# Coarse scores in four array quarters, coarse transposes in row halves, and a new opening order in a two-scale attention kernel

## The chip, the cores and the metric

The kernel runs on one core of one Trainium2 chip. The metric is the device time of one execution in microseconds (us). The engines are TensorE (PE, with its weight loads PEld), VectorE (DVE), ScalarE (ACT), GpSimd (POOL) and the queue SP, which only starts transfers.

## The reference

For 8 batches, 8 heads, 576 positions and a head dimension of 64:

```python
q_d, k_d, v_d = (t.reshape(B, H, 144, 4, D).mean(axis=3) for t in (q, k, v))
out_d = softmax(q_d @ k_d.T / 8) @ v_d                # coarse scale
out_up = repeat(out_d, 4, axis=2)
scores = where(abs(i - j) < 4, q @ k.T / 8, -1e9)     # local band
x = out_up + softmax(scores) @ v                      # heads joined to 512 columns
gate = sigmoid(sum(conv_w[k] * shifted(x, k) for k in range(5)))
out = (gate * (x @ w_val)) @ w_out
```

Weights come in as float64, the rest as float32.

## The kernel before

Work is cut into 32 pairs of heads, four to a batch; `p` counts pairs. For each pair TensorE makes: local scores (`sl`, a mask product and 40 small products), coarse scores (`sd`, six products of 64 rows by 64 columns by 144), transposes of the local weights (`tl0`, `tl1`) and of the coarse weights (`tc0`, `tc1`), the local values (`x`, 20 products) and the coarse values (`odp`). A product in float32 is two records in the trace (288 records on `sd` of 24 pairs). DVE takes the maxima (`mx`, `cmx`), subtracts, sums, adds local and coarse parts (`xt`) and does the convolution taps (`gp`); ACT does the exponentials and copies results out of PSUM (`pt`, `pdt`, `od`, `xh`, `hh`, `ob`); POOL shares the pooling, some normalisations and low parts (`xl`, `hl`) with DVE.

Behind the pairs run two projections in split precision: `val` = x by `w_val` and `out` = h by `w_out`, 256 chunks of six products (lines 864 to 866). The text calls a chunk P, as the order strings do. A chunk of `val` needs `xh` and `xl` of two pairs of its batch.

The coarse means of q and k come, for the first eight pairs, from DVE and POOL (`half`, `qd`); later ones, and all means of v, are summed by transfers: one load (`qs0`, `vs0`) and three accumulating transfers that POOL starts (line 401). `odp` of a batch waits for the third (`vs3`).

What sets the order: on TensorE two strings written out by hand. `FILL` gives the first ten pairs, 41 chunks among them; after it `STEADY` is repeated for each pair. On the other engines a planner orders operations by due times and lengths, with corrections by name (`BIAS`) and by instance (`DUE`). Each engine runs its list in order. Filler products (`keep_warm`, line 374) are put where the planner expects TensorE to stand idle.

PSUM has eight banks: three in rotation under the tag `s` (`sl`, `sd`, and two for `x`), two under `t` (`tl`, `tc`, `odp`), three under `v`. An operation that takes a bank waits until its last user has been read.

Of the kernel before, what the change touches and what calls it, by code (L numbers as in the profile page):

```python
# [8 lines left out]
F32 = mybir.dt.float32  # L9
# [28 lines left out]
LATE = {"qs": 9000, "vs": 7000}  # L38
# [3 lines left out]
ROWS, NG, GR = 112, 3, 48  # L42

LO, HI = slice(0, 64), slice(64, 128)
SB, TB, VB = 3, 2, 3
# [18 lines left out]
)  # L64
STEADY = "P P sl tc1' tc0' sd tl1' tl0' P P P P P P odp' x'"
# [5 lines left out]
    "pdt1": -8000, "h2.0": 2000, "hlo3.0": -1000, "norm1": 2000, "fld": 4000, "h2.1": -8000, "h3.0": -4000,  # L71
    "cwfld": 2000, "xl": -8000, "pvb": 2000, "od": -1000, "xt0": -2000, "exp": 1000, "rcp": -2000,
    "cexp0": -1000, "h1.1": 4000, "cmx0": -1000, "hhi3.0": -2000,
}
FIRST = {("qk", 0): -2e6, ("qk2", 0): -1.9e6}
DUE = {("raw", 0): -799008, ("vw", 0): -799729, ("raw", 2): 10251, ("qk", 1): -799570}
# [6 lines left out]
class Planner:  # L83
# [5 lines left out]
    LOAD = 1000  # L89
# [36 lines left out]
    def lat(self, o):  # L126
        return o["late"] or (self.LOAD if "SP" in o["opts"] else self.LAT)

# [34 lines left out]
    def simulate(self):  # L163
# [3 lines left out]
        self.recent, self.idle, self.port = [], {}, 0  # L167
# [17 lines left out]
        while events:  # L185
# [127 lines left out]
def tile_two_scale_attn_gated_conv(  # L313
# [9 lines left out]
    mask: bass.AP,  # L323
    out: bass.AP,
# [13 lines left out]
    ident = cpool.tile([P, P], F32, name="ident")  # L338
    ident_b = cpool.tile([P, P], BF16, name="ident_b")
# [31 lines left out]
    def keep_warm(bank):  # L371
        n = min(WARM, bank.shape[1])
        for _ in range(plan.warm):
            nc.tensor.matmul(
                out=bank[:, 0:n],
                lhsT=nc.const_aps.tensor(1.0, (P, bank.shape[0]), BF16),
                rhs=nc.const_aps.tensor(1.0, (P, n), BF16),
                start=True,
                stop=True,
            )  # L380
# [9 lines left out]
    def sums_in(b):  # L390
# [25 lines left out]
    def load(p):  # L416
# [670 lines left out]
```

## Time and profile before

| | |
|---|---|
| three runs | 419.21 us median, 416.21 to 419.66 |
| span of the profiled execution | 412.6 us |
| that execution's own time | not listed apart: the median is 6.6 us over the span, the fastest run 3.6 us |
| PE busy | 387.2 us, 94% |
| DVE, ACT, POOL busy | 306.3, 251.3, 140.4 us |
| moved by transfers | 68.00 MB, mean 165 GB/s |

The span runs from the first to the last instruction; what lies around it is in the runs' times and not in the profile. Busy shares are averages over an opening, a long regular stretch and a tail, so they are read by stretch. A PE record lasts longer than its slot, since products overlap: how long a step takes is the distance from its start to the start of the next step.

### The profile page before, as it was taken

To read this page: it belongs to the slowest core of one execution; us is meant where nothing else is said; L and a number is where in the kernel's file an instruction comes from. 1 tells how busy PE (TensorE), PEld (TensorE's weight loads), DVE (VectorE), ACT (ScalarE), POOL (GpSimd) and SP (SyncE) were. 2 spreads that over 40 slices of the span, in tenths; PEclk is the share of its full clock that TensorE was granted. 3 is DMA by queue.
4 is the path that set the end of the run, shared out by engine and by line. 5 is a ranking of instruction groups with operands and counts; after the bars stand their busy time and mean duration, and the time that the engine had idled before them with its cause. 6 is when DMAs were issued, how large, how long until landed. Compare 5 with 4: busy or idle time off the path is not lost.

```text
span 412.6 us, 15125 instructions
## 1 busy us (share of the span) xinstructions
PE 387.2 (94%) x6505; PEld 342.8 (83%) x6505; DVE 306.3 (74%) x650; ACT 251.3 (61%) x693; POOL 140.4 (34%) x159
## 2 busy tenths in 40 slices
PE   8664888989999999999999999999999999999996
PEld 5444656879998988888999989888888999998996
DVE  2676869989998976786689678786678668974730
ACT  1445677579667675566656665676556665675321
POOL 4563484365443322541154213432254112320000
PEclk9688698999999999999999999999999999999999
DMA  7987778668796479846994798667894431001002
GB/s 225 279 189 206 223 208 228 124 195 249 187 211 146 152 210 237 192 108 171 257 217 88 209 234 221 160 173 215 231 176 96 150 126 40 20 30 59 31 30 86
DMA packets 23603, 68.00 MB, mean 165 GB/s; under 512 B 3056, under 2 KB 4080, under 8 KB 23536
## 3 DMA queue, kind: packets, MB, share of 16 engines
q1 hardware_dynamic: 18352, 49.17, 36.7%
q0 software_dynamic: 4896, 17.70, 25.6%
q8 instruction: 51, 0.84, 0.8%
q10 hardware_dynamic: 288, 0.16, 0.1%
q14 instruction: 16, 0.13, 0.1%
HBM read 57.59 MB, written 9.44 MB: 162 GB/s over the span
## 4 chain that ended last, share of the span: by engine, by line
PE 82%; DMA 6%; DVE 5%; POOL 2%; ACT 2%; issue 1%; SPq 0%; ACTq 0%; POOLq 0%; DVEq 0%
PE out L864 9%; PE val L864 9%; PE out L865 8%; PE out L866 8%; PE val L866 8%; PE val L865 8%; PE sd L549 6%; PE sl L482 5%; PE x L671 5%; PE tl L621 5%; PE tc L644 5%; PE odp L708 5%; DMA raw_v<-in_w_val 3%; DMA qk<-in_qk 3%; PE sl L475 1%
## 5 line engine op out<-in xcount | busy, mean ns | idle before, releaser
L753 DVE SCALAR_TENSOR_TENSOR gp<-xt,cw,gp 128x576 f32<-128x576 f32 x128 | 109.8, 858 | 0.5 <-ACT gp L747 0.2
L864 PE MATMUL val<-xh,wh_v 128*128 128x288 f32 x256 | 79.4, 310 | 0.0
L864 PE MATMUL out<-hh,wh_o 128*128 128x288 f32 x256 | 78.8, 308 | 0.0
L866 PE MATMUL val<-xl,wh_v 128*128 128x288 f32 x256 | 76.0, 297 | 1.4 <-issue 1.1
L865 PE MATMUL val<-xh,wl_v 128*128 128x288 f32 x256 | 75.9, 297 | 0.0
L865 PE MATMUL out<-hh,wl_o 128*128 128x288 f32 x256 | 75.7, 296 | 0.0
L866 PE MATMUL out<-hl,wh_o 128*128 128x288 f32 x256 | 75.6, 295 | 0.0
L518 POOL TENSOR_TENSOR pexp<-ex,rs 64x350 f32<-64x350 f32 x38 | 44.1, 1159 | 78.5 <-DVE crs L587 26.5
L682 DVE TENSOR_TENSOR xt<-x,od 128x290 f32<-128x290 f32 x64 | 26.7, 452 | 37.1 <-PE x L671 35.9
L866 PEld LDWEIGHTS val<-xl,wh_v 128*128 128x128 f32 x256 | 48.4, 189 | 2.1 <-issue 1.3
L864 PEld LDWEIGHTS val<-xh,wh_v 128*128 128x128 f32 x256 | 48.4, 189 | 1.4 <-issue 0.4
L864 PEld LDWEIGHTS out<-hh,wh_o 128*128 128x128 f32 x256 | 48.1, 188 | 1.1 <-issue 0.2
L865 PEld LDWEIGHTS val<-xh,wl_v 128*128 128x128 f32 x256 | 48.5, 189 | 0.0
L865 PEld LDWEIGHTS out<-hh,wl_o 128*128 128x128 f32 x256 | 48.2, 188 | 0.0
L947 ACT ACTIVATE ob<-out 128x288 f32<-128x288 f32 x64 | 26.1, 407 | 36.3 <-PE out L866 33.2
L866 PEld LDWEIGHTS out<-hl,wh_o 128*128 128x128 f32 x256 | 48.0, 188 | 0.0
L626 ACT COPY pt<-tl 128x256 f32<-128x256 f32 (+1 forms) x64 | 25.9, 425 | 19.4 <-PE tl L621 19.4
L401 POOL DMA_DIRECT2D vs<-in_vgr x24 | 20.5, 865 | 47.6 <-PE sd L549 20.7
L571 ACT ACTIVATE pd<-sd,cbi 112x144 f32<-112x144 f32 x96 | 35.3, 376 | 1.8 <-DVE cbi L564 1.7
L651 ACT COPY pdt<-tc 72x336 f32<-72x336 f32 x64 | 25.2, 434 | 17.3 <-PE tc L644 17.2
L401 POOL DMA_DIRECT2D qs<-in_qkr x18 | 18.1, 1006 | 51.6 <-DMA qs<-in_qkr 24.6
L621 PE MATMUL tl<-ident,pexp 128*128 128x128 f32 x160 | 26.5, 290 | 8.9 <-POOL pexp L518 4.7
(83 smaller groups left out, 758.8 us busy)
## 6 DMA issues: line engine op xcount, KB each, us to landing
qk<-in_qk SPq DMA_DIRECT2D x31, 586.0 KB, 5.7
qs<-in_qkr POOLq DMA_DIRECT2D x18, 576.0 KB, 7.4
vw<-in_vw SPq DMA_DIRECT2D x32, 320.0 KB, 4.9
out_t<-ob SPq DMA_DIRECT2D x31, 288.0 KB, 3.7
vs<-in_vgr POOLq DMA_DIRECT2D x24, 288.0 KB, 5.5
qs<-in_qkr SPq DMA_DIRECT2D x6, 576.0 KB, 5.8
vs<-in_vgr SPq DMA_DIRECT2D x8, 288.0 KB
raw_v<-in_w_val SPq DMA_DIRECT2D x8, 256.0 KB, 4.7
```

What stands on the lines that cost most here:

```text
L401: nc.gpsimd.dma_start(out=u[nm][:, cs], in_=src[b, r][:, cs], accum_op=ALU.add)
L518: eng.tensor_tensor(out=px[r, :, BQ * e : BQ * e + KW], in0=s["ex"][r, :, 0:KW], in1=s["rs"][r].broadcast_to([64, NSB, KW]), op=ALU.mult,)
L571: nc.scalar.activation(out=s["pd"][:, g], in_=s["sd"][:, g], func=AF.Exp, scale=1.0 / 128.0, bias=s["bi"][:, g : g + 1], accum_out=s["csm" ...
L621: nc.tensor.transpose(out=tp[:, j], in_=s["px"][:, m : m + 2].rearrange("p a b -> p (a b)"), identity=ident)
L626: nc.scalar.copy(out=s["pt"][:, lo : lo + n], in_=s["tl", u])
L651: nc.scalar.copy(out=s["pdt"][:, kb], in_=s["tc", kb])
L682: nc.vector.tensor_tensor(out=s["xt"][:, 4:].rearrange("p (m a j r) -> p a m j r", m=NPR, a=2, r=2)[:, par], in0=s["x", par].rearrange("p ...
L753: nc.vector.scalar_tensor_tensor(out=s["gp"], in0=s["xt"][:, k : k + S], scalar=cw[:, c, k : k + 1], in1=s["gp"], op0=ALU.mult, op1=ALU.add,)
L864: nc.tensor.matmul(out=o, lhsT=wh[:, d, col], rhs=his[d][:, cs], start=d == 0, stop=False)
L865: nc.tensor.matmul(out=o, lhsT=wl[:, d, col], rhs=his[d][:, cs], start=False, stop=False)
L866: nc.tensor.matmul(out=o, lhsT=wh[:, d, col], rhs=los[d][:, cs], start=False, stop=d == NC - 1)
L947: nc.scalar.mul(t["ob"][:, cs], box[hf][:, ps_cs], 0.5)
```

## The change

- **Coarse scores.** The six products go to two banks at three places of 256 columns, in an order in which four neighbouring products use four different quarters of the array (rows low or high, columns low or high), then two more. Before, three rounds of two.
- **Coarse transposes.** `tc0` and `tc1` become one step `tc` of twelve transposes, each of 48 rows by 72 columns, low rows and high rows in turn, into two banks of tag `t`; the six before took 112 rows. ACT copies 288 columns twice in place of 336.
- **First batch's means of v.** A new step `vd` for pairs 0 to 3: six products of a constant 0/1 matrix (`pick`, 221 KB, loaded once) with the values already on chip, and an ACT copy. The load and three accumulating transfers of that batch are gone.
- **Banks.** Tag `s` keeps one bank for `sl`; a new tag `w`, one buffer of two banks, is shared by `sd` and `x`.
- **Order.** `FILL`, `BIAS` and `DUE` have new values, the planner's model of transfers is changed, and fillers before `tl` and `odp` use float32 ones.

```diff
-LATE = {"qs": 9000, "vs": 7000}
+LATE = {"qs": 2930, "vs": 1480}
+PLACE = (0, 2, 1, 0, 2, 1)
-SB, TB, VB = 3, 2, 3
+TB, VB = 2, 3
 FILL = (
-    "sl:0 sd:0 tl1:0 tc0:0 sl:1 tc1:0 sd:1 tl1:1 tl0:0 sl:2 sd:3 tc0:1 tc1:1 tl0:1 sl:4 odp:1 odp:0 sl:3 "
-    "x:1 tl1:2 x:0 sd:2 tl0:2 tc1:3 tl1:3 tl0:3 sd:4 x:2 tc0:2 tc1:2 odp:2 tl1:4 sl:5 P tc0:3 odp:3 tc1:4 "
-    "sd:5 x:3 tl0:4 P tc0:4 P P tc1:5 P P P sd:6 P x:4 P P odp:4 sl:6 tl0:5 P P tc1:6 tc0:6 P P sl:7 "
...
+    "sl:0 sd:0 sl:1 sd:1 tl0:0 tc:0 tl1:1 vd:0 sl:2 tl1:0 odp:0 sd:3 tc:1 tl0:1 vd:1 tl1:2 sl:4 odp:1 x:1 "
+    "sl:3 x:0 sd:2 P tl0:2 tl0:3 tl1:3 sd:4 x:2 tc:2 tl0:4 P vd:2 vd:3 odp:2 tl1:4 sl:5 tc:3 P x:3 odp:3 tc:4 "
+    "sd:5 tl1:5 P P P P sd:6 P odp:4 P sl:6 tc:5 P P odp:5 x:4 tc:6 sl:7 sd:7 odp:6 tl0:5 P P P sl:8 tl0:6 P "
...
-STEADY = "P P sl tc1' tc0' sd tl1' tl0' P P P P P P odp' x'"
+STEADY = "P P sl tc' sd tl1' tl0' P P P P P P odp' x'"
 BIAS = {
-    "pdt1": -8000, "h2.0": 2000, "hlo3.0": -1000, "norm1": 2000, "fld": 4000, "h2.1": -8000, "h3.0": -4000,
+    "pdt1": -6000, "h2.0": 5000, "hlo3.0": -9000, "norm1": 18000, "fld": 21000, "h2.1": -7000,
...
-            ("vs", vgr, [SD // 2, NC, 4, D], "odp", 820, 0),
+            ("vs", vgr, [SD // 2, NC, 4, D], "odp", 1100, 0 if b else NC),
...
-            sc = ps.tile([P, 3, SD], F32, tag="s", name=f"sd{p}", bufs=SB)
-            keep_warm(sc.rearrange("p a b -> p (a b)"))
+            w = ps.tile([P, 2, 512], F32, tag="w", name=f"sd{p}", bufs=1).rearrange("p a b -> p (a b)")
+            sc = w[:, 0:768].rearrange("p (i j) -> p i j", j=256)[:, :, 0:SD]
+            keep_warm(w[:, 0:512])
             q = s["qd"].rearrange("p a j -> p (a j)")
-            for i in range(3):
-                for r in (LO, HI):
-                    nc.tensor.matmul(
-                        out=sc[r, i],
-                        lhsT=q[r, 48 * i : 48 * i + 64],
+            for u in (0, 1, 4, 5, 2, 3):
+                h, j = divmod(u, 3)
+                r = LO if h == 0 else HI
+                nc.tensor.matmul(
+                    out=sc[HI if u % 2 else LO, PLACE[u]],
+                    lhsT=q[r, 48 * j : 48 * j + 64],
...
-    def coarse_transpose(p, kb):
+    def coarse_transpose(p):
...
+            for kb in range(2):
+                for n in range(NG):
+                    for e, r in enumerate((slice(0, GR), slice(64, 64 + GR))):
+                        nc.tensor.transpose(
+                            out=tps[e][:, kb, n],
+                            in_=s["pd"][r, PLACE[2 * n + e], half * kb : half * kb + half],
+                            identity=ident[r, r],
+                        )
...
+        for e in range(2):
+            op((f"pdt{e}", p), "ACT", 335, evac(e), [("tc", p)], free=[("odp", p - 2)])
...
+            w = ps.tile([P, 2, 512], F32, tag="w", name=f"x{p}", bufs=1)
             for par in range(2):
-                s["x", par] = ps.tile([P, NPR * GQ], F32, tag="s", name=f"x{par}_{p}", bufs=SB)
+                s["x", par] = w[:, par, 0 : NPR * GQ]
...
+    def value_sums(p):
...
+            for kb in range(2):
+                for n in range(3):
+                    nc.tensor.matmul(
+                        out=t[:, kb],
+                        lhsT=pick[:, 3 * kb + n],
+                        rhs=s["vw"][:, 2 * kb + n].rearrange("p h d -> p (h d)"),
+                        start=n == 0,
+                        stop=n == 2,
+                    )
...
+        op(("vd", p), "PE", 1330, mm, [("vw", p), ("pick", 0)], banks=[("t", [("vdc", p)])], cols=(3072, 256))
+        op(("vdc", p), "ACT", 320, evac, [("vd", p)])
```

**TensorE, one pair of the regular stretch.** Before:

```order
L475 LDWEIGHTS ident_b
L475 MATMUL sl_5009<-mask_b,ident_b 128x350
L482 MATMUL sl_5009<-qk_4443 29x35 x40
L644 MATMUL tc_1_5056<-ident,pd_4909 72x112 x3
L644 MATMUL tc_0_5063<-ident,pd_4909 72x112 x3
L549 MATMUL sd_5068<-qs_4064 64x144 x6
L621 MATMUL tl_1_5080<-ident,pexp_81 128x128 x2
L621 MATMUL tl_0_5083<-ident,pexp_81 128x128 x3
```

And with the change (five more pairs of `tc_0`, `tc_1` rows stand at the line of dots):

```order
L521 LDWEIGHTS ident_b
L521 MATMUL sl_5135<-mask_b,ident_b 128x350
L528 MATMUL sl_5135<-qk_4578 29x35 x40
L696 MATMUL tc_0_5183<-ident,pd_5037 72x48
L696 MATMUL tc_1_5184<-ident,pd_5037 72x48
...
L598 MATMUL sd_5199<-qs_4183 64x144 x6
L670 MATMUL tl_1_5213<-ident,pexp_82 128x128 x2
L670 MATMUL tl_0_5217<-ident,pexp_82 128x128 x3
```

The place of `tc`, `sd` and `tl` is the same; both banks of `tc` are now filled in turn, where `tc_1` was full after three of six.

**TensorE in the opening, up to the first coarse values.** Before, twenty fillers (the last is the first row here) stand ahead of `odp` of pairs 1 and 0, which read `vs`:

```order
L374 LDWEIGHTS const-bfloat16-1.0
L374 MATMUL odp_626<-const-bfloat16-1.0 128x144
L708 MATMUL odp_626<-pdt_497,vs_215 64x144 x4
L708 MATMUL odp_656<-pdt_284,vs_215 64x144 x4
L475 LDWEIGHTS ident_b
L475 MATMUL sl_663<-mask_b,ident_b 128x350
L482 MATMUL sl_663<-qk_241 29x35 x40
L671 MATMUL x_1_718<-pt_407,vw_268 64x58 x2
```

With the change (`vd` reads `vw` and `pick`, `odp` reads `vd`):

```order
L426 MATMUL tl_1_374<-ones_r 128x256 x5
L670 MATMUL tl_1_374<-ident,pexp_81 128x128 x2
L799 MATMUL vd_384<-vw_193,pick 72x128 x6
L521 LDWEIGHTS ident_b
L521 MATMUL sl_398<-mask_b,ident_b 128x350
L528 MATMUL sl_398<-qk_268 29x35 x40
L670 MATMUL tl_1_448<-ident,pexp_80 128x128 x2
L766 MATMUL odp_456<-pdt_356,vd_440 64x144 x4
L598 MATMUL sd_466<-qd_83 64x144 x6
```

The first `odp` now stands after three `sl` instead of four, and waits for no transfer of its own.

**SP's queue, the first loads.** Before:

```order
L424 DMA qk_129<-in_qk 128x2x290
L424 DMA qk_129<-in_qk 128x2x296
L429 DMA vw_186<-in_vw 128x640
L424 DMA qk_188<-in_qk 128x1172
L826 DMA raw_v_199<-in_w_val 128x256
L396 DMA vs_215<-in_vgr 72x1024
L424 DMA qk_221<-in_qk 128x1172
L424 DMA qk_241<-in_qk 128x1172
L429 DMA vw_268<-in_vw 128x640
L429 DMA vw_274<-in_vw 128x640
L826 DMA raw_v_282<-in_w_val 128x256
```

With the change:

```order
L470 DMA qk_132<-in_qk 128x2x290
L470 DMA qk_132<-in_qk 128x2x296
L470 DMA qk_135<-in_qk 128x1172
L475 DMA vw_193<-in_vw 128x640
L909 DMA raw_v_201<-in_w_val 128x256
L475 DMA vw_218<-in_vw 128x640
L470 DMA qk_268<-in_qk 128x1172
L1075 DMA pick<-in_sums 128x432
L475 DMA vw_304<-in_vw 128x640
L470 DMA qk_321<-in_qk 128x1172
L470 DMA qk_358<-in_qk 128x1172
```

The second pair's `qk` moved up by one, `pick` came in, the first batch's `vs` went out.

## Rows read from the trace of the kernel before

**Rows 1.** The page: span, busy time by engine, the granted TensorE clock in 40 slices.

```profile
span 412.6 us, 15125 instructions
PE 387.2 (94%) x6505; PEld 342.8 (83%) x6505; DVE 306.3 (74%) x650; ACT 251.3 (61%) x693; POOL 140.4 (34%) x159
PEclk9688698999999999999999999999999999999999
```

**Rows 2.** Busy time by stretch: stretch, its length, busy us (instructions) of PE, PEld, DVE, ACT, POOL, then granted clock, share of the DMA engines, GB/s.

```profile
0.00:60.00 60.00, 42.57 (x820) 30.55 (x821) 36.35 (x88) 31.76 (x99) 31.43 (x58) 0.83 0.83 222
70.00:126.00 56.00, 54.20 (x896) 47.30 (x894) 52.89 (x108) 39.84 (x109) 26.02 (x25) 1.00 0.79 191
126.00:370.00 244.00, 243.91 (x4340) 220.68 (x4339) 191.95 (x410) 158.11 (x435) 77.87 (x71) 1.00 0.63 161
```

**Rows 3.** The same view for the part before pair 3's `xt` is done, in two pieces.

```profile
0.00:40.00 40.00, 26.01 (x456) 18.12 (x458) 21.69 (x55) 16.26 (x52) 18.99 (x44) 0.84 0.87 226
40.00:66.40 26.40, 21.40 (x444) 16.57 (x442) 20.26 (x46) 19.68 (x58) 15.43 (x19) 0.82 0.78 222
```

**Rows 4.** The chain of waits, shares of the span by engine.

```profile
PE 82%; DMA 6%; DVE 5%; POOL 2%; ACT 2%; issue 1%; SPq 0%; ACTq 0%; POOLq 0%; DVEq 0%
```

**Rows 5.** The timeline of PE over one pair of the regular stretch: start us, length us, line, operation, count.

```profile
201.28 0.71 PE L708 MATMUL odp<-pdt,vs 72*64 72x144 f32 x8
201.92 0.81 PE L671 MATMUL x<-pt,vw 64*64 64x58 f32 x40
202.66 0.40 PE L864 MATMUL out<-hh,wh_o 128*128 128x288 f32 x1
...
204.62 0.89 PE L482 MATMUL sl<-qk 64*29 64x35 f32 x80
205.44 0.77 PE L644 MATMUL tc<-ident,pd 112*72 112x112 f32 x6
206.14 0.95 PE L549 MATMUL sd<-qs 64*64 64x144 f32 x12
207.02 0.77 PE L621 MATMUL tl<-ident,pexp 128*128 128x128 f32 x5
207.54 0.38 PE L864 MATMUL val<-xh,wh_v 128*128 128x288 f32 x1
...
215.85 0.89 PE L482 MATMUL sl<-qk 64*29 64x35 f32 x80
```

**Rows 6.** What ACT and DVE do around that pair, and ACT two pairs later, by their timelines.

```profile
205.96 0.77 ACT L651 COPY pdt<-tc 72x336 f32<-72x336 f32 x2 [0.55 <-PE tc L644]
```

```profile
202.83 0.83 DVE L682 TENSOR_TENSOR xt<-x,od 128x290 f32<-128x290 f32 x2 [1.94 <-PE x L671]
```

```profile
232.82 0.21 ACT L571 ACTIVATION_READ_ACCUMULATOR pd<-sd,cbi 112x1 f32 x1
```

**Rows 7.** PE's timeline around that later pair: `sd`, the `tl` behind it, and `x`.

```profile
228.60 0.95 PE L549 MATMUL sd<-qs 64*64 64x144 f32 x12
229.49 0.77 PE L621 MATMUL tl<-ident,pexp 128*128 128x128 f32 x5
...
235.62 0.81 PE L671 MATMUL x<-pt,vw 64*64 64x58 f32 x40
```

**Rows 8.** PE's timeline in the opening; in brackets the idle time ahead and what ended it.

```profile
13.90 0.69 PE L621 MATMUL tl<-ident,pexp 128*128 128x128 f32 x2 [4.27 <-DVE pexp L518]
...
25.93 0.77 PE L621 MATMUL tl<-ident,pexp 128*128 128x128 f32 x5 [3.67 <-POOL pexp L518]
...
32.98 1.48 PE L374 MATMUL odp<-const-bfloat16-1.0 128*128 128x144 bf16 x20
39.50 2.19 PE L708 MATMUL odp<-pdt,vs 72*64 72x144 f32 x16 [5.04 <-DMA vs<-in_vgr]
...
46.69 0.54 PE L374 MATMUL x<-const-bfloat16-1.0 128*128 128x290 bf16 x3 [1.73 <-DVE xt L682]
...
59.78 0.40 PE L864 MATMUL val<-xh,wh_v 128*128 128x288 f32 x1
...
70.28 0.40 PE L866 MATMUL val<-xl,wh_v 128*128 128x288 f32 x1
```

**Rows 9.** The page on the DMA queues (packets, MB, share of 16 engines) and on one kind of transfer (count, KB each, us to landing).

```profile
q1 hardware_dynamic: 18352, 49.17, 36.7%
q0 software_dynamic: 4896, 17.70, 25.6%
...
vs<-in_vgr POOLq DMA_DIRECT2D x24, 288.0 KB, 5.5
```

**Rows 10.** The three longest transfers on the chain of waits in the first 100 us: start us, length us.

```profile
7.91 11.95 DMA raw_v<-in_w_val
...
28.01 6.68 DMA qk<-in_qk
...
44.14 3.64 DMA raw_o<-in_w_out
```

More of the change, by code (lines that the diff above doesn't have):

```diff
@@ L126, in lat @@
     def lat(self, o):
-        return o["late"] or (self.LOAD if "SP" in o["opts"] else self.LAT)
+        return self.LAND + (o["late"] or 0) if o["late"] or "SP" in o["opts"] else self.LAT
     def switch(self, a, b):
@@ L638, in mm, with evac, run @@
         def mm():
-            if "pdt" not in s:
-                s["pdt"] = work.tile([half, 2, NG, ROWS], F32, tag="pdt", name=f"pdt{p}")
-            s["tc", kb] = tp = ps.tile([half, NG, ROWS], F32, tag="t", name=f"tc{p}_{kb}", bufs=TB)
-            keep_warm(tp.rearrange("p a b -> p (a b)"))
-            for i in range(NG):
-                nc.tensor.transpose(
-                    out=tp[:, i],
-                    in_=s["pd"][:, i, half * kb : half * kb + half],
-                    identity=ident[0:ROWS, 0:ROWS],
-                )
-        def evac():
-            nc.scalar.copy(out=s["pdt"][:, kb], in_=s["tc", kb])
-        op(
-            (f"tc{kb}", p), "PE", 340, mm, [("cnorm", p)],
-            banks=[("t", [(f"pdt{kb}", p)])], cols=(588, 336),
-        )
-        op((f"pdt{kb}", p), "ACT", 371, evac, [(f"tc{kb}", p)], free=[("odp", p - 2)])
+            tps = [
+                ps.tile([half, 2, NG, GR], F32, tag="t", name=f"tc{p}_{e}", bufs=TB) for e in range(2)
+            ]
+            s["tc"] = tps
+            keep_warm(tps[0].rearrange("p a b c -> p (a b c)"))
+            for kb in range(2):
[5 more added lines that the diff above has]
+                            identity=ident[r, r],
+                        )
+        def evac(e):
+            def run():
+                if "pdt" not in s:
+                    s["pdt"] = work.tile([half, 2, NG, 2, GR], F32, tag="pdt", name=f"pdt{p}")
+                nc.scalar.copy(out=s["pdt"][:, :, :, e], in_=s["tc"][e])
+            return run
+        op(
+            ("tc", p), "PE", 430, mm, [("cnorm", p)],
+            banks=[("t", [(f"pdt{e}", p)]) for e in range(2)], cols=(588, 288),
+        )
+        for e in range(2):
+            op((f"pdt{e}", p), "ACT", 335, evac(e), [("tc", p)], free=[("odp", p - 2)])
     def local_av(p):
@@ L691, in local_av @@
         op(("x", p), "PE", 760, mm, deps,
-           banks=[("s", [(f"xt{par}", p)]) for par in range(2)], cols=(1160, 290))
+           banks=[("w", [("xt0", p), ("xt1", p)])], cols=(1160, 290))
         for par in range(2):
@@ L989, in cw_value, with pick_in @@
         nc.vector.tensor_copy(out=cw2, in_=cw_parts[3]["a"].bitcast(F32))
+    def pick_in():
+        nc.sync.dma_start(out=pick, in_=sums)
+    op(("pick", 0), "SP", 700, pick_in)
     op(("cwf", 0), "SP", 120, cw_in)
@@ L1003, in tile_two_scale_attn_gated_conv @@
             local_transpose(p, u)
-        for kb in range(2):
-            coarse_transpose(p, kb)
+        coarse_transpose(p)
+        if p < NC:
+            value_sums(p)
         local_av(p)
```

113 lines of the change are left out of this document (73 added, 40 removed), and 36 rows, old and new, of tables (BIAS, DUE, FILL).

## The prediction

> **What bounds the kernel now.** I read the page first [rows 1]: PE is busy 94% of 412.6 us and DVE 74%. A mean does not say where the time lies, so next come the stretches [rows 2]. From 126 to 370 us PE is busy 243.91 of 244.00 us at the full granted clock (1.00, the 2.4 GHz level), DVE 79% and ACT 65%: TensorE alone sets the pace, and what leaves it there leaves the end. From 70 to 126 us PE is busy 97% and DVE 94%: two engines near their limit. In the first 60 us PE is busy 42.57 us, fillers among them, at a mean granted clock of 0.83, so part of it at 1.2 GHz, with the DMA engines at 0.83: that stretch is made of waits. The chain of waits says the same [rows 4]: PE 82%, DMA 6%, DVE 5%.
>
> The regular pair [rows 5] shows the prices: 11.23 us from one `sl` to the next (215.85 - 204.62), in it `odp` 0.64 (to the start of `x`), `x` 0.74, `tc` 0.70, `sd` 0.88, `tl` 0.52. The opening [rows 8] shows PE idle 4.27, 3.67, 5.04 and 1.73 us in front of four steps. The first chunk of `val` starts at 59.78, and the first that needs pair 3 at 70.28. From there the work runs nearly without a gap, so I call 70.28 the end of the opening. Behind it stand 26 `sd` and 27 `tc`.
>
> **Coarse scores.** `odp` and `sd` stream the same 144 columns, two products side by side: `odp` has eight records, four rounds, 0.64 us; `sd` has twelve, six rounds, 0.88 us [rows 5]. A round costs (0.88 - 0.64) / 2 = 0.12 us. With four products side by side the twelve records make two rounds of four and two of two: four rounds, 0.64 us, a gain of 0.24. That four quarters do run together shows `x`, which uses all four: 40 records in 0.74 us, 0.074 for a round of four, where 40 one by one at even half of that would take 1.48. If the four do not overlap, the gain is 0. I take 0.24.
>
> **Coarse transposes.** No row shows two transposes side by side, so I bound them. Now: six in 0.70 us, 0.117 each for 112 columns. A round of `sd` takes 0.147 for 144, so 32 columns cost 0.030, and 48 columns would take 0.117 - 64 x 0.00094 = 0.057. Six rounds of two: 0.34 us, if streaming is the limit. But each half must load its own 72 columns of weights, twelve loads for six. `x` loads 64 columns for each record and needs 0.074 a round although its 58 columns would stream in 0.066: scaled to 72 columns, 0.083 a round, 0.50 us. Without overlap, twelve of 0.057 make 0.68; if a half costs what a whole costs now, 1.40. I take 0.50, from the nearest row with loads as short, a gain of 0.20. The Trainium skill ("TensorE: Matmul & The Clock Gate", LDWEIGHTS) says that a load's time goes by its columns and not by its rows, 60 ns for 72: halving the rows would save nothing on loads, and twelve in a row would take 0.72 us. The rows of `x` agree only that loads to different quarters overlap.
>
> **A wait behind it.** `tl` reuses both banks of `tc`. ACT's first copy began 0.29 us after the third transpose had started (205.96 against 205.44 + 2 x 0.117), and two copies took 0.77 [rows 6]. Now both banks fill together: the last round starts at 0.42 us after the first, the copies begin at 0.71 and take 0.77 x 288 / 336 = 0.66, so the second bank is free at 1.37, about 1.41 with a hand-over. TensorE would want it at 0.50 + 0.64 + 2 x 0.104 = 1.35. A wait of 0.06 us, so a pair gains 0.44 - 0.06 = 0.38. With `tc` at 0.34 the same sum gives 0.50; with no gain in `tc`, 0.24. Times 27 pairs: **10 us**, between 6.5 and 13.5.
>
> **One buffer for `sd` and `x`.** In the regular stretch this costs nothing: `xt` is done at 203.66 [rows 6], 2.5 us before `sd` starts at 206.14 [rows 5]; the exponentials of the latest case end at 233.03 [rows 6], 2.6 us before `x` at 235.62 [rows 7]. Should those covers go, each pair would wait for the difference. In the opening it costs once, where `x` of pair 2 now stands right behind `sd` of pair 4: from the end of `sd` to the last exponential it took 233.03 - 229.49 = 3.5 us [rows 6, 7].
>
> **Value sums.** `vd` is twelve records of 128 columns over the whole array; `tl` runs five such in 0.52 us [rows 5], 0.104 each, so 1.25 us and 0.16 of lead, 1.4 us, four times 5.6 us (twice that at 1.2 GHz). All four stand before the end of the opening, where PE waits [rows 8]; if that cover were gone they would cost 5.6 us. In return `odp` no longer waits for the accumulated `vs`: TensorE had nothing but twenty fillers from 32.98 and began at 39.50, so **6.5 us** of wait go, if nothing else is late there. What is late next is pair 2's and 1's weights (`pexp`) and `xt`, which DVE and POOL make. The transfers also lighten: accumulating ones moved 17.70 MB in 25.6% of 412.6 us, 168 GB/s of all engines' time, plain ones 49.17 MB in 36.7%, 325 GB/s [rows 9]. Out go 0.295 MB plain and three times that accumulated, 0.9 + 5.3 us; in comes `pick`, 0.22 MB, 0.7 us. That is 5.5 us of transfer time, in a stretch with the DMA engines 0.87 busy [rows 3] and 22.3 us of transfers on the chain [rows 10].
>
> **The opening.** Bounds: DVE is busy 21.69 + 20.26 = 42 us before pair 3's `xt` is done at about 66.4 [rows 3] and starts near 5.5, so with the same work it can't be done before 47.5: at most 19 us. At the other end nothing is gained and the 3.5 us wait is lost. I take 6.5 + 5.5 - 3.5 = **8.5 us**, since the wait and the transfers are rows of their own, and the new order of the loads can only move what is behind them.
>
> Sum: 412.6 - 10 - 8.5 = 394.1 us of span. The median of the runs is 6.6 us over the profiled span, whose own time is not listed; with that, **401 us**.
>
> **Rivals.**
> - The opening gains nothing: when `vs` is gone, the next input (weights as float64, `qk`, DVE's own list) is as late. For it: DVE is 94% busy from 70 to 126 us and could hold what PE gains; DMA is 0.83 busy. Then 412.6 - 10 + 6.6 = 409 us, up to 413 with the new wait. Chance 0.27.
> - The scores don't overlap by four, so the change doesn't do what it says. The Trainium skill ("TensorEngine Tiling (Array Packing)", Restrictions and Gotchas) has it that different row tiles can't access one PSUM bank at the same time; here low and high rows write both banks. In rows: `sd` would stay at 0.88 or more, the pair gains 0.20, 27 x 0.20 = 5.4, and 412.6 - 5.4 - 8.5 + 6.6 = 405 us. Against it: the old `sd` writes one bank from both row halves, and a round of two took 0.12 us like `odp`'s [rows 5]. By that, the trace disagrees with the rule for different partitions of a bank. Chance 0.06.
> - The opening gains more than I say, up to DVE's limit: 388 to 395 us. For it: DVE is idle 24 of the first 60 us [rows 2]. Chance 0.08.
> - **Slower.** The row halves don't run together and each costs what a whole transpose costs, 0.117 us: `tc` takes 1.40, the pair loses 0.70 and gains 0.24. 27 x 0.46 = 12.4 us lost; with no gain in the opening 412.6 + 12.4 + 6.6 = 432, with 8.5 us 423. It decides from 0.94 / 12 = 0.078 us a half. For it: twelve loads for six. Against it: `x` has shorter products and four loads a round in 0.074. Chance 0.05.
>
> **How the numbers follow.** My forecast has 0.54, with its own range of 394 to 409 us (419.2 less 6.5 to 13.5 in the regular part and 4 to 12 in the opening). To leave out no more than 2 in 10 the range takes in the empty opening and part of the better one: 391 to 412. A measurement of this kernel tells about 1% from no change, that is 415 to 423. Faster: 0.54 + 0.06 + 0.08 and most of the empty opening, 0.90. Same: the rest of that and half of the slow rival's better case, 0.06. Slower 0.04.
>
> **What would show it.** In the regular stretch `sl` to `sl` should fall from 11.23 to 10.85 us, `sd` to 0.64, `tc` to 0.50, with an idle PE of some 0.06 us before the second part of `tl`, released by `pdt`. No wait of PE on `xt` or on the exponentials should stand there. In the opening `odp` should not wait for a transfer, the first chunk that needs pair 3 should start near 62 us in place of 70.28, and one wait of about 3.5 us should stand in front of `x` of pair 2. I am wrong if `sd` keeps six rounds, if `tc` exceeds 0.94 us, or if PE idles in the regular stretch by more than a few tenths a pair.

## The result and the profile after

The changed kernel takes 401.75 us in the median of four runs (398.22 to 408.58), the kernel before 418.12 in four (416.21 to 419.66): 0.957 (95% interval 0.949 to 0.965), faster. Run again beside other kernels (`after_again` below, with a profile of its own) it took 0.969 (0.960 to 0.978). The profiled executions of `banks_alone` (438.4 us) and `pool_later` (410.1) were the longest of their kernel's runs; those of `vd_old_order` and `pool_later_again` were disturbed throughout (13.12 and 33.87 us from one `sl` to the next) and are not read.

The profiled execution took 399.65 us, 1.75 us more than its span; in every run that lists both, the difference is 1.7 to 1.8. So the span of 412.6 before [rows 1] stands for a run of 414.4 us.

The page of the changed kernel:

```profile
span 397.9 us, 15570 instructions
PE 373.1 (94%) x6715; PEld 331.5 (83%) x6715; DVE 303.1 (76%) x627; ACT 260.7 (66%) x725; POOL 146.3 (37%) x170
```

Busy time by stretch, in the columns of [rows 2]:

```profile
70.00:116.00 46.00, 42.23 (x836) 37.06 (x835) 40.23 (x83) 33.10 (x95) 23.02 (x23) 1.00 0.82 213
116.00:350.00 234.00, 231.43 (x4461) 210.33 (x4457) 193.84 (x390) 165.55 (x453) 84.16 (x79) 0.99 0.65 170
```

TensorE bounds the long stretch as before [rows 2], but no longer without gaps: 2.57 of 234 us are idle (before 0.09 of 244), and from 70 to 116 us 3.77 of 46 (before 1.80 of 56).

The timeline of PE over one regular pair, to set beside [rows 5]:

```profile
208.44 0.32 PE L521 MATMUL sl<-mask_b,ident_b 128*128 128x350 bf16 x1
...
209.51 0.45 PE L696 MATMUL tc<-ident,pd 48*72 48x48 f32 x12
209.89 0.72 PE L598 MATMUL sd<-qs 64*64 64x144 f32 x12
210.54 0.76 PE L670 MATMUL tl<-ident,pexp 128*128 128x128 f32 x5
...
216.01 0.71 PE L766 MATMUL odp<-pdt,vs 72*64 72x144 f32 x8
216.65 0.81 PE L729 MATMUL x<-pt,vw 64*64 64x58 f32 x40
219.09 0.32 PE L521 MATMUL sl<-mask_b,ident_b 128*128 128x350 bf16 x1
```

`tc` takes 0.38 us (before 0.70), `sd` 0.65 (before 0.88), and nothing stands in front of `tl`. In this `sd` the twelve records start in groups of four, four, two and two, the first four within 20 ns. The pair takes 10.65 us, which is also the median from pair 11 on; before it was 11.23.

Where TensorE waited, over the whole span (us in total, times, longest):

```profile
PE x L426 <- ACT pd L620: 3.6, 1, 3.6
PE tl L426 <- ACT pdt L706: 2.6, 4, 0.8
PE sd L426 <- ACT pd L620: 2.4, 1, 2.4
PE tc L696 <- issue: 2.2, 1, 2.2
PE x L729 <- issue: 1.8, 2, 1.3
PE sl L528 <- issue: 1.6, 3, 0.8
```

Three of these are waits for banks (`x` and `sd` on the exponentials `pd`, in the two banks that they now share; `tl` on `pdt`, since `tc` now fills both banks of tag `t`); in the other three the profile names nothing that was waited for.

The opening on PE's timeline, to set beside [rows 8]:

```profile
18.05 1.47 PE L799 MATMUL vd<-vw,pick 128*72 128x128 f32 x12
20.80 0.71 PE L766 MATMUL odp<-pdt,vd 72*64 72x144 f32 x8
...
45.36 1.52 PE L426 MATMUL x<-const-bfloat16-1.0 128*128 128x290 bf16 x8 [3.62 <-ACT pd L620]
...
52.38 3.02 PE L799 MATMUL vd<-vw,pick 128*72 128x128 f32 x24
55.33 0.71 PE L766 MATMUL odp<-pdt,vd 72*64 72x144 f32 x8
...
64.76 0.40 PE L949 MATMUL val<-xl,wh_v 128*128 128x288 f32 x1 [0.18 <-DVE xl L824]
```

The first coarse values come at 20.80 in place of 39.50, but the first chunk that needs `xl` of pair 3 only 5.5 us earlier (64.76 against 70.28), and in the second profile of the changed kernel 1.7 (68.59).

**Where the 14.7 us of span are.** Two points have the same work of TensorE behind them in both kernels: the start of `sl` of pair 10, where `FILL` ends, and of pair 31, the last. Before, and after:

```profile
125.73 0.32 PE L475 MATMUL sl<-mask_b,ident_b 128*128 128x350 bf16 x1
...
361.95 0.32 PE L475 MATMUL sl<-mask_b,ident_b 128*128 128x350 bf16 x1
```

```profile
119.26 0.32 PE L521 MATMUL sl<-mask_b,ident_b 128*128 128x350 bf16 x1
...
347.70 0.32 PE L521 MATMUL sl<-mask_b,ident_b 128*128 128x350 bf16 x1
```

6.5 us are won by pair 10, 7.8 between the two, 0.5 behind. The ten `sd` (0.23) and nine `tc` (0.32) ahead of pair 10 are worth 5.2, so the opening itself gave 1.3 us. In the second profile pair 10 starts at 122.13, 2.9 us later, and by the same sum the opening lost 1.6: it gained nothing that two profiles can tell. The 21 pairs between should give 12.2; one of them takes 14.24 us, two others 0.3 and 0.7 more than 10.65, and before one took 0.3 more: with some hundredths elsewhere, 4.4 us given back.

The long pair, on DVE, POOL, ACT and PE:

```profile
127.07 4.18 DVE L836 SCALAR_TENSOR_TENSOR gp<-xt,cw,gp 128x576 f32<-128x576 f32 x1
131.18 0.81 DVE L740 TENSOR_TENSOR xt<-x,od 128x290 f32<-128x290 f32 x2
```

```profile
121.69 0.83 POOL L447 DMA_DIRECT2D vs<-in_vgr  x1 [2.72 <-DMA vs<-in_vgr]
...
127.44 1.06 POOL L564 TENSOR_TENSOR pexp<-ex,rs 64x350 f32<-64x350 f32 x1
128.18 2.45 POOL L987 TENSOR_TENSOR hl<-h,hh 128x576 fp32r<-128x576 f32 x2
```

```profile
132.02 0.67 ACT L820 CAST xh<-xt 128x576 fp32r<-128x576 f32 x1 [3.27 <-DVE xt L740]
...
133.61 0.67 ACT L706 COPY pdt<-tc 72x288 f32<-72x288 f32 x2
```

```profile
132.14 0.72 PE L598 MATMUL sd<-qs 64*64 64x144 f32 x12 [0.65 <-DVE xt L740]
134.13 0.75 PE L670 MATMUL tl<-ident,pexp 128*128 128x128 f32 x5 [1.27 <-ACT pdt L706]
```

A tap that takes 0.81 us elsewhere took 4.18 and ended 0.6 us after POOL's three operations (131.25 against 128.18 + 2.45 = 130.63). `xt` came late, `sd` waited for the shared buffer, ACT made `xh`, `hh` and a tap ahead of `pdt`, and `tl` waited for `pdt`. The granted clock was 0.54 from 134.5 to 138 us, the 1.2 GHz level in most of it: 14 products at 0.24 us in place of 0.13, 1.5 us more.

### The profile page after: what moved, and what is told of

Same layout as the page of the kernel before. It is cut to its first block, busy times and chain, and to the rows that moved or that the text cites. A ratio compares the mean times of both kernels' runs of the same rounds, so it can differ in the third digit from the quotient of the medians.

```text
span 397.9 us, 15570 instructions
## 1 busy us (share of the span) xinstructions
PE 373.1 (94%) x6715; PEld 331.5 (83%) x6715; DVE 303.1 (76%) x627; ACT 260.7 (66%) x725; POOL 146.3 (37%) x170
## 4 chain that ended last, share of the span: by engine, by line
PE 87%; DVE 4%; ACT 3%; DMA 2%; issue 2%; SPq 0%; DVEq 0%; ACTq 0%
PE out L947 10%; PE val L947 9%; PE out L949 9%; PE out L948 9%; PE val L949 9%; PE val L948 8%; PE sl L528 6%; PE x L729 6%; PE tl L670 5%; PE sd L598 5%; PE odp L766 5%; PE tc L696 3%; DMA qk<-in_qk 2%; PE sl L521 1%; PE sd L426 1%
## 5 line engine op out<-in xcount | busy, mean ns | idle before, releaser
L836 DVE SCALAR_TENSOR_TENSOR gp<-xt,cw,gp 128x576 f32<-128x576 f32 x128 | 115.9, 908 | 0.2
L564 POOL TENSOR_TENSOR pexp<-ex,rs 64x350 f32<-64x350 f32 x44 | 49.2, 1119 | 76.5 <-DVE crs L636 28.0
L947 PEld LDWEIGHTS out<-hh,wh_o 128*128 128x128 f32 x256 | 48.9, 191 | 1.4 <-issue 0.4
L948 PEld LDWEIGHTS out<-hh,wl_o 128*128 128x128 f32 x256 | 49.0, 192 | 0.0
L949 PEld LDWEIGHTS out<-hl,wh_o 128*128 128x128 f32 x256 | 48.9, 191 | 0.0
L447 POOL DMA_DIRECT2D qs<-in_qkr x18 | 15.8, 879 | 51.6 <-DMA qs<-in_qkr 36.7
L824 DVE TENSOR_TENSOR xl<-xt,xh 128x576 fp32r<-128x576 f32 x27 | 22.0, 816 | 16.1 <-ACT xh L820 16.1
L447 POOL DMA_DIRECT2D vs<-in_vgr x21 | 17.9, 851 | 44.4 <-DMA vs<-in_vgr 36.5
L528 PEld LDWEIGHTS sl<-qk 64*29 64x29 f32 x2560 | 25.3, 103 | 8.6 <-issue 6.4
```

The costliest lines, as they stand in the source:

```text
L447: nc.gpsimd.dma_start(out=u[nm][:, cs], in_=src[b, r][:, cs], accum_op=ALU.add)
L528: nc.tensor.matmul(out=sc[32 * qd : 32 * qd + BQ, i * KW : (i + 1) * KW], lhsT=t[r, 0, blk : blk + BQ], rhs=t[r, 1, blk : blk + KW], start ...
L564: eng.tensor_tensor(out=px[r, :, BQ * e : BQ * e + KW], in0=s["ex"][r, :, 0:KW], in1=s["rs"][r].broadcast_to([64, NSB, KW]), op=ALU.mult,)
L836: nc.vector.scalar_tensor_tensor(out=s["gp"], in0=s["xt"][:, k : k + S], scalar=cw[:, c, k : k + 1], in1=s["gp"], op0=ALU.mult, op1=ALU.add,)
L947: nc.tensor.matmul(out=o, lhsT=wh[:, d, col], rhs=his[d][:, cs], start=d == 0, stop=False)
L948: nc.tensor.matmul(out=o, lhsT=wl[:, d, col], rhs=his[d][:, cs], start=False, stop=False)
```

## The experiments

| kernel | `sl` of pair 10 starts | regular pair | ratio to before (95%) |
|---|---|---|---|
| before | 125.73 | 11.23 | 1 |
| changed | 119.26 | 10.65 | 0.957 (0.949 to 0.965) |
| `sd_by_two` | 123.03 | 10.89 | 0.977 (0.967 to 0.986) |
| `tc_apart` | 120.31 | 10.77 | 0.967 (0.952 to 0.982) |
| `steps_alone` | 159.63 | 10.83 | 1.054 (1.044 to 1.064) |
| `banks_alone` | 149.69 | 11.21 | 1.042 (1.034 to 1.051) |
| `vs_by_transfers` | 136.51 | 10.65 | 0.990 (0.979 to 1.000) |
| `vd_old_order` | not read | not read | 1.012 (1.004 to 1.020) |
| `old_tables` | 127.30 | 10.94 | 0.989 (0.981 to 0.996) |
| `pool_later` | 119.71 | 10.65 | 0.961 (0.951 to 0.971) |
| `after_again` | 122.13 | 10.66 | 0.969 (0.960 to 0.978) |
| `pool_later_again` | not read | not read | 0.964 (0.957 to 0.971) |
| `vd_in_wait` | 117.94 | 10.65 | 0.971 (0.964 to 0.979) |
| `code_shifted` | 121.34 | 10.65 | 0.968 (0.962 to 0.975) |

The two rows of the same kernel, `changed` and `after_again`, differ by 0.012 in the ratio and by 2.9 us at pair 10; differences of that size between other rows tell nothing. The regular pair repeats to 0.01 us.

**Coarse scores in rounds of two (`sd_by_two`).** The reads behind `sd` follow its places:

```diff
-            for u in (0, 1, 4, 5, 2, 3):
+            for j in range(3):
+                for r in (LO, HI):
...
-                    out=sc[HI if u % 2 else LO, PLACE[u]],
+                        out=sc[r, j],
...
```

> The changed kernel with one part undone: the six products of the coarse scores go in rounds of two (low rows to low partitions, high rows to high partitions) as in the kernel before; banks, transposes, order and tables stay. Theory A (the steady gain is the sum of two shorter steps, each paid in full because TensorE bounds the regular stretch): sd goes from 0.65 back to 0.88 us, sl to sl from 10.65 to 10.88 us, and over some 27 pairs the time rises by 6 us, 401 to about 407. Rival B (the steady pair is bound by what waits behind, so that a longer sd is hidden): sd 0.88 but sl to sl under 10.75, time within 2 us of the changed kernel. Rival C (sd was short for another reason than four quarters): sd stays near 0.65.

PE's timeline, one regular pair:

```profile
216.36 0.95 PE L597 MATMUL sd<-qs 64*64 64x144 f32 x12
217.24 0.44 PE L669 MATMUL tl<-ident,pexp 128*128 128x128 f32 x2
```

`sd` is back at 0.88, the pair at 10.89, and the median at 408.8 us, 7 us over the changed kernel (0.977 of the kernel before, against 0.957 and 0.969): theory A. Four quarters are the gain, and a regular pair gives it in full.

**Row halves one after the other (`tc_apart`).**

```diff
-            for kb in range(2):
-                for n in range(NG):
-                    for e, r in enumerate((slice(0, GR), slice(64, 64 + GR))):
+            for e, r in enumerate((slice(0, GR), slice(64, 64 + GR))):
+                for kb in range(2):
+                    for n in range(NG):
```

> The changed kernel with the twelve coarse transposes in another order: the six of the low rows first, then the six of the high rows, so that neighbours share their rows of the array; the same twelve loads and twelve streams. Theory A (tc is 0.38 us because two row halves run side by side, a round being 0.042): a round becomes one transpose, tc takes twelve times 0.042 or more, 0.50 to 0.70 us, sl to sl rises by 0.12 to 0.32, the time by 3 to 9 us. Rival B (the halves are short because the weight loads overlap anyway, side by side or not, and the stream of 48 columns sets the pace of each alone): tc stays at 0.38 to 0.45 and the time within 2 us. Rival C (loads bind when nothing runs beside them, a half costs the 0.117 us of a whole transpose before): tc 1.40, sl to sl +1.0, time +25 us.

```profile
169.32 0.57 PE L696 MATMUL tc<-ident,pd 48*72 48x48 f32 x12
169.82 0.72 PE L598 MATMUL sd<-qs 64*64 64x144 f32 x12
```

`tc` takes 0.50 us, the pair 10.77: 0.12 more, theory A at its lower end by the rows; as time, 0.967, it isn't told apart from the changed kernel. In the trace three of the twelve still start within 7 ns of another, so some run side by side even in this order, and 0.12 is a lower bound of what that gives. Rival C is out.

**The steps without the rest (`steps_alone`).** The steps and banks are those of the change; in the order one `tc` stands in place of `tc0` and `tc1`:

```diff
 FILL = (
-    "sl:0 sd:0 tl1:0 tc0:0 sl:1 tc1:0 sd:1 tl1:1 tl0:0 sl:2 sd:3 tc0:1 tc1:1 tl0:1 sl:4 odp:1 odp:0 sl:3 "
+    "sl:0 sd:0 tl1:0 sl:1 tc:0 sd:1 tl1:1 tl0:0 sl:2 sd:3 tc:1 tl0:1 sl:4 odp:1 odp:0 sl:3 "
...
```

> The kernel before with only the two shorter steps and their banks (sd in four quarters, tc in twelve halves, one bank for sl, two shared by sd and x); the old order of the first ten pairs, the old tables and the old model of transfers, value sums of the first batch by transfers as before. Theory A (all that lasts is the steady gain of 0.58 us a pair, and what the new opening wins is given back between 70 and 135 us): it takes back nearly the whole difference, 403 to 406 us against 418 before and 402 with the whole change. Rival B (the prediction's split: 10 us from the steps, 8.5 from the opening): 408 to 410. Rival C (the shared banks cost waits in the old order that the new order was made to avoid): 410 to 418, with waits of x on the exponentials and of sd on xt in the opening.

Its PE timeline between 50 and 80 us:

```profile
56.33 1.15 PE L375 MATMUL x<-const-bfloat16-1.0 128*128 128x290 bf16 x4 [2.66 <-DVE xt L695]
...
67.55 1.37 PE L375 MATMUL sd<-const-bfloat16-1.0 128*128 128x350 bf16 x8 [1.67 <-ACT pd L575]
...
74.10 2.09 PE L375 MATMUL x<-const-bfloat16-1.0 128*128 128x290 bf16 x8 [4.53 <-ACT pd L575]
```

440 us, outside all three expectations. The regular pair has the gain (10.83, with 0.17 for two fillers ahead of `tl`), but pair 10 starts 34 us later than before. The waits are those of rival C, far beyond its price; the granted clock from 40 to 80 us is 0.59.

**The banks without the steps (`banks_alone`).**

```diff
-            sc = ps.tile([P, 3, SD], F32, tag="s", name=f"sd{p}", bufs=SB)
+            w = ps.tile([P, 2, 512], F32, tag="w", name=f"sd{p}", bufs=1)
+            sc = w[:, 0, 0 : 3 * SD].rearrange("p (a b) -> p a b", b=SD)
...
-                s["x", par] = ps.tile([P, NPR * GQ], F32, tag="s", name=f"x{par}_{p}", bufs=SB)
+                s["x", par] = w[:, par, 0 : NPR * GQ]
```

> The kernel before with one thing changed: the banks. sl has one bank, sd and x share one buffer of two (sd uses its first bank, six products in rounds of two as before), and the coarse weights get a third buffer; transposes, orders and tables stay. Theory A (the shared banks are what made the two steps alone 21 us slower: each x waits for the exponentials of the sd ahead of it and each sd for the xt of the x ahead): the opening loses 30 us or more as there (TensorE's tenth pair starts near 159 us in place of 126), sl to sl stays 11.23, and the time is 440 plus 27 times 0.4, about 450 us. Rival B (that loss came from the steps or from the two steps meeting the old tables): 417 to 425 us.

433 us, 17 less than expected, but theory A in kind: with the old steps, order and tables the shared banks alone cost 4.2%. In its profiled execution (438.4 us; the other three took 431.8 to 434.4) pair 10 starts 24 us later than before, and `x` waits 4.98, 2.51 and 3.95 us for the exponentials.

**The first batch's value sums by transfers (`vs_by_transfers`).**

```diff
-            ("vs", vgr, [SD // 2, NC, 4, D], "odp", 1100, 0 if b else NC),
+            ("vs", vgr, [SD // 2, NC, 4, D], "odp", 1100, 0),
...
```

> The changed kernel with the value sums of the first batch undone: they come again from one load (put where the load of the 0/1 matrix stood) and three accumulating transfers, the steps vd are gone, the order of TensorE is otherwise the new one. Theory A (vd removed a wait of 6.5 us and 5.5 us of transfers at the price of up to 7 us of TensorE work of which part stands in waits): the first odp waits again for the third transfer, first odp near 30 us in place of 20.8, and the time rises by 6 to 12 us. Rival B (the opening is bound by DVE and by other loads, vd's own 24 products at the lower clock cost as much as they save): time within 2 us of the changed kernel.

```profile
35.90 1.23 PE L766 MATMUL odp<-pdt,vs 72*64 72x144 f32 x8 [14.69 <-DMA vs<-in_vgr]
```

414 us in the median, 12 over the changed kernel (0.990 against 0.957 and 0.969); pair 10 starts 17 us later than in the first profile of the changed kernel and 14 later than in the second. Theory A, and more: the first `odp` comes at 35.90, not near 30, and where it stands early, as it now does, the sums by transfer cost 14 to 17 us there.

**Value sums by TensorE in the old order (`vd_old_order`).**

```diff
-... sl:2 sd:3 tc0:1 tc1:1 tl0:1 sl:4 odp:1 odp:0 ...
+... sl:2 vd:0 sd:3 tc0:1 tc1:1 tl0:1 vd:1 sl:4 odp:1 odp:0 ...
...
```

> The kernel before with one thing added: the value sums of the first batch by TensorE (vd for pairs 0 and 1 ahead of the first coarse values, for pairs 2 and 3 ahead of their own), its 0/1 matrix loaded, the four transfers of that batch gone; banks, steps, order and tables otherwise as before. Theory A (the prediction's: 6.5 us of wait and 5.5 us of transfers go): the wait of odp for the transfer is gone and the time is 405 to 413 us. Rival B (in the old order pair 2's and 1's weights and DVE are as late): 416 to 421. Rival C (the vd steps, 1.4 us each and twice that at the lower clock, stand on the path): 422 to 430.

420.5 us, inside rival B's range, but 1.2% over the kernel before in the same comparison (415.3), which leans to rival C. In the old order, with tables made without it, `vd` brings nothing: theory A, a step of the prediction, falls. Whether other inputs are as late there (B) or the `vd` steps stand on the path (C) stays open.

**The old correction tables (`old_tables`).** `BIAS` and `DUE` are those of the kernel before.

> The changed kernel with the two correction tables (by name and by instance) of the kernel before; TensorE's order, steps, banks and vd stay. Theory A (TensorE's new order and vd carry the opening; the tables trim single waits): 402 to 407 us, the regular pair 10.65 or 10.83 if fillers come back. Rival B (the tables are what keeps DVE, ACT and POOL in step with the shared banks): 412 to 430, with waits of x on exponentials and of sd on xt in the first 120 us as in the run of the two steps alone.

410 us (0.989), between the two theories: pair 10 starts 8 us later than in the first profile with the new tables (5 than in the second), and each regular pair has float32 fillers ahead of `tl`, 0.28 us, 10.94.

**POOL's transfers behind its arithmetic (`pool_later`, `after_again`, `pool_later_again`).**

```diff
+AFTER = {
+    ("vs", 1, 3): [("hlo1.0", 1)], ("vs", 2, 3): [("hlo3.0", 1), ("norm0", 10)], ("vs", 3, 3): [("xl", 9)],
+}
...
-[(f"{nm}{r - 1}", b)], late=LATE[nm])
+[(f"{nm}{r - 1}", b)] + AFTER.get((nm, r, b), []), late=LATE[nm])
```

> The changed kernel with one edit: on POOL the three accumulating transfers of the fourth batch's value sums stand behind some of its arithmetic (the low parts of h and one of xh) instead of ahead of it, so POOL does not sit 6.5 and 2.7 us in front of a landing between 110 and 122 us. Theory A (that wait pushed three POOL operations back to back into 127 to 131 us, where one convolution tap on DVE then took 4.18 us in place of 0.81, xt came late, ACT's copies of the coarse transposes stood behind it, and TensorE stopped 0.65 and 1.27 us and fell to the lower clock): the pair that took 14.25 us takes 10.65 to 11, and the time falls by 3 to 3.5 us to about 398. Rival B (the tap is long for another reason, or another step is as late): the stop stays or moves, time within 1.5 us of the changed kernel.

> The changed kernel itself, unaltered, beside the next three on one chip, so that they are compared with it and not only with the kernel before. All theories: ratio to the kernel before as measured first, 0.95 to 0.965; the pair after the tenth again near 14 us long.

> The kernel with POOL's three accumulating transfers behind its arithmetic once more, with more rounds beside the changed kernel: its first profile had the long pair at 11.33 us in place of 14.24, but two other stops of some 4 us in that one execution. Theory A (the stop near 131 us was caused by POOL's wait and it was on the path): 2 to 3.5 us under the changed kernel. Rival B (TensorE makes it up elsewhere, or another stop comes with it): within 1.5 us.

The wait of `tl` in that pair, in the profile of `pool_later` that is read:

```profile
133.01 0.39 PE L429 MATMUL tl<-ones_r 128*128 128x256 f32 x1 [0.42 <-ACT pdt L709]
```

No tap there is longer than 1.85 us (4.18 and 4.76 in the two profiles of the changed kernel), `sd` does not wait, and the pair takes 11.33 us against 14.24 and 12.01, not the 10.65 to 11 of theory A. `after_again` misses its expectation of 14 us, and it shows why a long tap need not make a long pair: its tap of 4.76 us stands behind `xt`, and no step of TensorE waits for it (1.1 of the 12.01 us are a wait on `ob`). In `code_shifted`, with POOL's list unchanged, a tap of 3.80 us behind `xt` stands in a pair of 10.91. In `tc_apart` no tap there is over 2.20, but `pexp` on DVE takes 3.23 beside POOL ahead of `xt`, and the pair takes 14.85. So the chain of causes fits the rows where the long operation stands ahead of `xt`. As time the first comparison gives 0.961 and the second 0.964, against 0.957 and 0.969 of the changed kernel: no difference that these runs can tell. (The profiled execution of `pool_later` has two stops elsewhere, 4.07 us in `sl` at 168.05 and 3.78 in `tl` at 315.49.) Theory A is not shown for the time.

**`vd` in the wait of `x` (`vd_in_wait`).**

```diff
-sd:4 x:2 tc:2 tl0:4 P vd:2 vd:3 odp:2
+sd:4 vd:2 vd:3 x:2 tc:2 tl0:4 P odp:2
```

> The changed kernel with vd of pairs 2 and 3 moved up in TensorE's order, from behind the first chunk that follows tc of pair 2 to ahead of x of pair 2, where TensorE waits 3.6 us for the exponentials of sd of pair 4. Theory A (that wait, the 3.5 us of the prediction, is on the path and the 3.0 us of vd behind it fit into it): odp of pair 2 starts 2.5 to 3 us earlier and the time falls by 2 to 3 us. Rival B (what bounds the stretch is DVE and ACT, so the opening ends when it did): within 1 us. Rival C (ACT's copies of vd come between its exponentials and x waits longer, or the tables no longer fit the order): slower by 1 to 5 us.

```profile
44.40 0.79 PE L426 MATMUL x<-const-bfloat16-1.0 128*128 128x290 bf16 x5 [1.19 <-ACT pd L620]
...
48.77 0.71 PE L766 MATMUL odp<-pdt,vd 72*64 72x144 f32 x8
...
81.69 0.47 PE L426 MATMUL sl<-const-bfloat16-1.0 128*128 128x350 bf16 x2 [4.04 <-DVE ex L544]
```

The wait falls to 1.19 us, and `odp` of pair 2 starts at 48.77 in place of 55.33: 6.6 us earlier (58.94 in the second profile: 10.2), with most of the time at the lower clock there gone (granted clock 0.94 from 30 to 60 us, 0.77 in the changed kernel). Up to 81.69 us `sl` of pair 8 then waits 4.04 us for DVE, which must empty the one bank of `sl`; the chain of waits passes there through a load of `w_out` (65.42, 6.52 us) and DVE. Pair 10 starts 1.3 us earlier than in the first profile of the changed kernel and 4.2 earlier than in the second, which differ by 2.9 themselves; the ratio, 0.971, shows no gain. Theory A is right at its place, rival B at the end.

**TensorE's code moved by 72 places (`code_shifted`).**

```diff
+            if p == 0:
+                one = nc.const_aps.tensor(1.0, (P, 32), BF16)
+                for _ in range(40):
+                    nc.tensor.matmul(out=sc[0:32, 0:32], lhsT=one, rhs=one, start=True, stop=True)
+                plan.warm -= 4
```

> The changed kernel with 40 products of 32 columns in place of four of the twelve fillers at the very start, so that all later instructions of TensorE stand 72 places later in its stream, with the same work in the same order. Theory A (the stops inside a step, which the profile gives to issue and which end 1.2 to 1.6 us after a transfer of 16 KB on the queue of instructions, are TensorE waiting for its next block of code): the stops move: the one after five of the twelve transposes near 72 us no longer stands there but some 36 products earlier in the program, or goes, and likewise the ones in sl near 79 and 85 and in x near 98 us. Rival B (they are waits for data or banks): they stay after the same products. The time changes by less than 4 us either way.

In the changed kernel `x` stops after ten records, in its second profile (the second fence) too:

```profile
98.39 0.44 PE L729 MATMUL x<-pt,vw 64*64 64x58 f32 x10
99.33 0.46 PE L729 MATMUL x<-pt,vw 64*64 64x58 f32 x16 [0.50 <-issue]
```

```profile
100.53 0.44 PE L729 MATMUL x<-pt,vw 64*64 64x58 f32 x10
102.20 0.68 PE L729 MATMUL x<-pt,vw 64*64 64x58 f32 x30 [1.24 <-issue]
```

With the code shifted that `x` runs through, and a stop stands in a `tc` that had none:

```profile
98.54 0.81 PE L734 MATMUL x<-pt,vw 64*64 64x58 f32 x40 [0.20 <-ACT pd L625]
...
294.36 0.28 PE L701 MATMUL tc<-ident,pd 48*72 48x48 f32 x4
295.43 0.36 PE L701 MATMUL tc<-ident,pd 48*72 48x48 f32 x8 [0.78 <-issue]
```

The four named stops are gone from their products, as theory A has it. The second profile of the changed kernel lacks the ones in `tc` and `sl` too, so of the four it is the one in `x` that tells. The median, 400.73 us, is not told apart from the changed kernel's.

## Why the prediction came out right

401 us were predicted and 401.75 measured, well inside the range. The mechanism of the regular stretch was right; that the number is this close is luck, for it comes from terms that err in opposite ways.

- **Coarse scores: right.** 0.64 predicted, 0.65 measured, and 0.88 when the four quarters are taken back. The rival by the rule on banks of the Trainium skill ("TensorEngine Tiling (Array Packing)", Restrictions and Gotchas) is out for this layout: by the trace, low and high rows write both banks at the same time, in different partitions (four records start within 20 ns, `sd` takes 0.65 us).
- **Coarse transposes: mis-sized.** The step "0.083 a round" scaled a round of `x` with its four loads to a round of two. A round took 0.042 us, so `tc` is 0.38 and not 0.50, near the lower bound of 0.34 that streaming gave. The slower rival, decided from 0.078 us a half, is out.
- **The wait of 0.06 behind `tc`: absent** in the regular pair, because `tc` and `sd` together took 1.03 us and ACT's copies ended 1.18 after `tc` began (the row below, 210.00 + 0.69 against 209.51), by the time `tl` needed its second bank. The cover is thin: planned with the old tables, two fillers stand there.

```profile
210.00 0.69 ACT L706 COPY pdt<-tc 72x288 f32<-72x288 f32 x2 [0.27 <-PE tc L696]
```

- **Per pair 0.58 in place of 0.38.** Over ten `sd` and nine `tc` ahead of pair 10 and 21 pairs behind, that is 5.2 + 12.2 = 17.4 us (15.7 for the 27 pairs that the prediction counted) where 10 were predicted; 4.4 of it are given back in single stops.
- **Value sums: right in price.** 1.4 us each; 1.31 from the first `vd` to the next `sl`, and 2.95 for two ahead of 55.33, at a granted clock of 0.91.
- **The opening: the step that failed.** 8.5 predicted, 1.3 measured and -1.6 by the second profile; of all cases its first rival, "the opening gains nothing", describes it best. The first chunk that needs pair 3 came at 64.76 and 68.59, not near 62. The sum 6.5 + 5.5 - 3.5 put a wait, some transfers and one new wait side by side, as if each had a price of its own. The new wait came out right (3.62), and `odp` did lose its wait. But `vd` is worth nothing in the old order (`vd_old_order`) and 14 to 17 us in the new one (`vs_by_transfers`), and the shared banks, priced at that one wait, cost 24 us at pair 10 in the old order (`banks_alone`). That the new order and tables pay for the banks is read from the changed kernel as a whole: no run has the new order without the shared banks, and that four quarters need two banks was not tried either.
- **What is late next** was named (DVE, transfers) and not priced. `vd_in_wait` shows it: of 6.6 us or more won at 55 us, 1.3 to 4.2 are left at pair 10 and none that the times can tell.
- **What lies around the span: wrong.** 6.6 us were added, measured are 1.75: the profile before came from an execution 4.9 us under the median. The span was predicted at 394.1 and is 397.9, so the forecast lands on the median partly because the assumed surplus hid a span gain 3.8 us too large.

How the opening's 40 us between `steps_alone` and the changed kernel split between order, tables and `vd` is settled only one at a time (tables 5 to 8 us, `vd` 14 to 17, each taken out alone). The rest was not tried in parts.

## What to carry to other kernels

Where one engine runs without gaps, price a step by its own rows and believe the sum; both steps paid in full there. Where a stretch is made of waits, terms don't add: ask for each freed wait which buffer, engine or load is late next, and expect the same edit to be worth nothing or 14 us and more, depending on the order around it. An edit that shares buffers must be priced together with the order that it stands in, and a profile's span is set against that execution's own time, not against the median.

## What the runs showed of the hardware

**TensorE stops at the edges of its code.** The page of the changed kernel on the queue of instructions (transfers, MB, share):

```profile
q8 instruction: 53, 0.87, 0.9%
```

The trace has 13,557 instructions of TensorE (products, loads and 127 others) for 53 transfers of 16 KB, so a transfer carries 256 of 64 bytes; before, 51 for 13,104. The stop after five of twelve transposes:

```profile
71.74 0.32 PE L696 MATMUL tc<-ident,pd 48*72 48x48 f32 x5
74.28 0.33 PE L696 MATMUL tc<-ident,pd 48*72 48x48 f32 x7 [2.21 <-issue]
```

One such transfer ran from 71.42 to 72.70, and TensorE went on 1.58 us after it. In the twelve profiles that are read, TensorE stands idle 31 times behind 10 us for a reason that the profile gives to `issue`. All 31 stand at the same place of its stream counted modulo 256, after 193 to 195 instructions, and end 0.95 to 1.63 us after a transfer of that queue; and each time the transfers that had ended are exactly as many as the whole 256s that TensorE had behind it (eight at its instruction 2241, the stop above). In `code_shifted` place and count are the same and the product is another. Where the transfer had ended earlier, nothing stops: in the first profile of the changed kernel TensorE came to the other places, all but one, 1.7 us or more behind their transfer (that one 1.26, with 0.28 us lost). So TensorE waits there for its next instructions. Behind 60 us the stops of over 0.4 us cost 5.3 us beyond the usual distance of two products in that profile (2.4, 1.0, 0.5, 0.7, 0.7), 2.7 in the second and 1.2 in that of before; the longest, 4.3, is in `pool_later`. Many stand in `tc`, `sl` and `x`, steps of many short instructions; why some transfers come so late was not tried. The Trainium skill ("Runtime: NRT & Kernel Launch", Instruction fetch mechanics) says that crossing a 16 KiB boundary is mostly hidden: by the rows most of the 53 are, and six in the first profile are not, the five above and one at 32.44 us.

**A tap on DVE can last as long as POOL's work.** 4.18 us in place of 0.81 where POOL ran three operations back to back, and no such tap there with POOL's list rearranged. Eight of the twelve profiles have one tap of over 3 us (3.57 to 4.90), each beside three to six operations of POOL without a gap, and all eight end 0.62 or 0.63 us after the last of these. In the profile of before the longest tap was 2.51.
